# Matmuls on zeros at the head of an attention and MLP kernel: some bf16 ones exchanged for small float32 ones

## The chip, the cores and the metric

The kernel runs on one core of a Trainium2 chip. The metric is the device time of one execution in microseconds (us); the kernel before takes 675.98 us, the median of 3 runs (675.64 to 676.66). Profile times count from the first instruction of the profiled execution.

## The reference

Attention over 2 x 8 heads of 768 positions and 64 dimensions, in which a key counts for a query only if both fall in the same bucket (the signs of six projections), followed by two MLPs on the 1536 joined tokens:

```python
q_bits = (einsum('bhsd,dk->bhsk', q, proj) > 0); k_bits = (einsum('bhsd,dk->bhsk', k, proj) > 0)
mask = bucket(q_bits)[:, :, :, None] == bucket(k_bits)[:, :, None, :]
scores = where(mask, q @ k.T / sqrt(D), -1e9)
attn = exp(scores - max(scores)); attn = attn / (sum(attn) + 1e-9)
x = (attn @ v), heads joined to 512 columns
x = maximum(maximum(x @ w1, x @ w2), x @ w3) @ w_out
h = x @ w_in;  g = h where h >= 1, 0 where h <= -1, else (h + 1)**2 / 4
out = g @ w_out2
```

## The kernel before

Operands are split into a high and a low part, so that a float32 product becomes several products in TensorE's faster format. The attention comes first, in tiles of 128 queries by 768 keys, six to a head; then the MLPs, a long even stream of 128x512 matmuls (L867, L994).

A tile is computed by `t_qk` (L386 to L400): for each half of 384 keys a product of `qa` with `lo` (L395) and one of `qb` with `hi` (L398), into one half of a tile `s_ps`. VectorE takes the row maximum and copies (`t_max`, L402), ScalarE the exponential (`t_exp`, L416). In the odd heads and head 0 TensorE transposes the tile (`t_tr`, L425) into `t_ps` and multiplies it with V into `u_ps` (`g_pv`, L476). In the seven other heads, called turned, VectorE transposes 32x32 squares, and `block4` (L450) multiplies the whole head at once: 24 key blocks, each with four calls of 32 rows by 64 columns against 192 columns (L456, L457), which write to four places, one per group of 32 rows: `quarter(q)` is `u_ps`, the two halves of `t_ps`, and `pj_ps` (L447). `u_ps`, `pj_ps` and each half of `t_ps` are PSUM tiles of 128 x 512 float32.

The order of TensorE's work in the attention is written out by hand (L793 to L818); a planner places the other engines' work by costs and due times that it is given, and none of them comes from the matmuls on zeros. Each engine runs its own instructions in order.

The head of the kernel (L568 to L593) is apart from the planner. It issues the loads of head 0 and others on SyncE's queue, then 20 matmuls on zeros (`warm_up`, L285, a 128x256 bf16 tile `warm` by its first half), and prepares head 0: ScalarE makes `hi`, VectorE `lo`, TensorE multiplies with the projections (`bits_mm`, L368, rows 64 to 128 of `pj_ps` for the first half and of `u_ps` for the second), VectorE turns rows 64 to 108 of these into bits (`bits_rows`, L374), and VectorE and GpSimd move the parts to their rows (`prep_move`, L354). In the first tile `t_qk` puts 4 matmuls on zeros ahead of each L395 and 7 ahead of each L398 (L394, L397), written to the half of `t_ps` of the same number. Nothing reads what the matmuls on zeros write. All this is written under a manual schedule: the program keeps the written order on each engine, and waits are put in where one instruction touches what another has written or read.

At the end of the attention `g_fold_now` (L510) reads the two row halves of `u_ps` on two engines:

```python
nc.scalar.copy(out=pr["u"][DOWN, cs], in_=u_ps[UP, 0:HALF])            # L512
nc.vector.tensor_copy(out=pr["uc"][DOWN, cs], in_=u_ps[DOWN, 0:HALF])  # L513
```

Here `UP` is rows 0 to 64, `DOWN` rows 64 to 128, and `HALF` is 384.

Of the kernel before, what the change touches and what calls it, by code (L numbers as in the profile page):

```python
# [22 lines left out]
HALF = S // 2  # L23
# [90 lines left out]
def lsh_attention_moe_kernel(  # L114
# [14 lines left out]
    nc = tc.nc  # L129
# [20 lines left out]
    warm = const.tile([128, CH], BF16, name="warm")  # L150
# [5 lines left out]
    f32 = lambda ap: ap.bitcast(F32)  # L156
# [105 lines left out]
    def attention(mlp_steps):  # L262
        with ExitStack() as ax, ExitStack() as sx:
# [21 lines left out]
            def warm_up(count, i):  # L285
                for _ in range(count):
                    nc.tensor.matmul(out=t_ps[:, i, 0:CH], lhsT=warm[:, 0:128], rhs=warm, start=True, stop=True)


            def load_head(h, parts=1):  # L290
                r = raw_p.tile([128, S], F32, tag="r", name="r")
                for i in range(parts):
                    cs = slice(i * S // parts, (i + 1) * S // parts)
                    nc.sync.dma_start(out=r[:, cs], in_=kq[h, :, cs])
                    if parts > 1 and i == 0:
                        nc.sync.dma_start(out=pj_raw, in_=pj)
                head.setdefault(h, {})["r"] = r

            def load_v(h):
                vr = v_p.tile([128, NK, D], F32, tag="vr", name="vr", bufs=1)  # L300
                nc.sync.dma_start(out=vr, in_=v[h])
                head.setdefault(h, {})["vr"] = vr
# [45 lines left out]
            UP, DOWN = slice(0, 64), slice(64, 128)  # L348
# [37 lines left out]
            def t_qk(n, bank):  # L386
                h, t = divmod(n, NK)
                hd = head[h]
                qs = slice(t * 128, (t + 1) * 128)
                for half in range(2):  # L390
                    ks = slice(half * HALF, (half + 1) * HALF)
                    o = s_ps[bank.at][:, half, 0:HALF]
                    if n == 0:
                        warm_up(4, half)  # L394
                    nc.tensor.matmul(out=o, lhsT=hd["qa"][:, qs], rhs=hd["lo"][:, ks], start=True, stop=False)  # L395
                    if n == 0:
                        warm_up(7, half)  # L397
                    nc.tensor.matmul(  # L398
                        out=o, lhsT=hd["qb"][0:76, qs], rhs=hd["hi"][0:76, ks], start=False, stop=True
                    )  # L400
# [46 lines left out]
            def quarter(q):  # L447
                return (u_ps, t_ps[:, 0], t_ps[:, 1], pj_ps)[q]
# [118 lines left out]

            load_head(0, 2)  # L568
            nc.sync.dma_start(out=ident, in_=idn)
            warm_up(20, 0)  # L570
            load_v(0)
            load_head(1)
            banks0 = (pj_ps, u_ps)
# [97 lines left out]
            def tile_tasks(n):  # L671
# [4 lines left out]
                sp, pp = place("s", 1), place("p", 1 if turned else 2)  # L676
                takes = own(sums_p, "sums", h // 2, 1)
                qk = task("PE", 0.72, m, t_qk, n, sp, after=ready[h], takes=[sp], leaves=[h_place[h]])
                mx = task("DVE", 1.04, m, t_max, n, sp, after=[qk], takes=[pp], leaves=[sp])
                ex = task("ACT", 1.13, m, t_exp, n, after=[mx], takes=takes, lag=0.1)  # L680
# [342 lines left out]
    with tc.manual_schedule():  # L1023
        nc.scalar.dma_start(out=pc_sb, in_=pc)
        nc.vector.memset(half_sb, 0.5)
        nc.vector.memset(sc_sb[0:64], 1.0)
        nc.vector.memset(sc_sb[64:128], SCALE)
        mlp_steps = mlp()
        attention(mlp_steps)
        for _ in mlp_steps:  # L1030
            pass
# [42 lines left out]
```

## Time and profile before

| | |
|---|---|
| median of 3 runs | 675.98 us (675.64 to 676.66) |
| the profiled execution | 676.23 us, span 674.4 us from first to last instruction |
| TensorE | 662.3 us busy (98%), 4440 matmuls and as many weight loads |
| VectorE, ScalarE, GpSimd | 73%, 50%, 41% busy |
| attention, MLPs | to about 213 us, from there to the end |

In the timeline PE is TensorE's matmuls and PEld its weight loads; DVE is VectorE, ACT ScalarE, POOL GpSimd, SPq the issue of DMAs. A row gives start, duration and how many instructions were merged, then the engine, the line of the kernel and the tiles. The brackets give how long the engine stood idle before and what released it; "issue" means that it waited for nothing the profile shows. A matmul's duration goes on past the start of the next, as they are pipelined: the pace is read from the starts.

### The profile page before, as it was taken

The numbers are of one execution on the slowest core, as the hardware profiler recorded it, in microseconds if no ns is written. First come the engines' busy times: TensorE is split into PE (matmuls) and PEld (weight loads), VectorE is DVE, ScalarE is ACT, GpSimd is POOL, SyncE is SP. The second block draws the span as 40 slices with busy tenths as digits, with TensorE's granted clock in tenths as the row PEclk, the third lists the DMA queues.
The fourth block names the chain that finished last, engine by engine and source line by source line (L and its number), as shares of the span: only waits on it lengthen the run. The fifth ranks groups of instructions, "written<-read, shape, count | busy, mean of one in ns | idle before, by whom it ended". The sixth has DMA issues, their size and how long they took to land.

```text
span 674.4 us, 11567 instructions
## 1 busy us (share of the span) xinstructions
PE 662.3 (98%) x4440; PEld 530.3 (79%) x4440; DVE 492.3 (73%) x725; ACT 337.3 (50%) x625; POOL 273.4 (41%) x247
## 2 busy tenths in 40 slices
PE   8999999999999999999999999999999999999998
PEld 5667777677776888888888888888888888888886
DVE  6788889989962668777444366765888888888844
ACT  3686876887883233233222234765444444444430
POOL 4427448458322244354232123643444444444430
PEclk9999999999999999999999999999999999999999
DMA  4866777777431222221111121111222121111005
GB/s 126 218 163 159 200 190 208 206 193 180 108 118 49 94 94 94 95 88 52 52 56 33 63 94 62 63 63 33 66 76 73 67 64 63 63 63 62 33 0 188
DMA packets 27855, 66.99 MB, mean 99 GB/s; under 512 B 4164, under 2 KB 9124, under 8 KB 27800
## 3 DMA queue, kind: packets, MB, share of 16 engines
q1 hardware_dynamic: 27656, 66.25, 33.9%
q8 instruction: 35, 0.57, 0.3%
q14 instruction: 20, 0.16, 0.1%
q10 hardware_dynamic: 144, 0.00, 0.0%
HBM read 46.17 MB, written 3.19 MB: 73 GB/s over the span
## 4 chain that ended last, share of the span: by engine, by line
PE 94%; DVE 2%; DMA 2%; ACT 1%; issue 1%; SPq 0%; DVEq 0%; ACTq 0%
PE b L867 49%; PE b L994 19%; PE s_ps L395 5%; PE u_ps L480 5%; PE t_ps L428 5%; PE s_ps L398 4%; PE u_ps L456 3%; PE pj_ps L369 2%; PE t_ps L456 1%; DVE p L405 1%; DVE lo L329 1%; DMA r<-in_kq 1%; DMA rb<-d 0%; ACT pt L438 0%; PE pj_ps L456 0%
## 5 line engine op out<-in xcount | busy, mean ns | idle before, releaser
L867 PE MATMUL b<-x_hl,wx 128*128 128x512 f32 x684 | 159.6, 389 | 0.0
L867 PEld LDWEIGHTS b<-x_hl,wx 128*128 128x128 f32 x684 | 128.4, 188 | 26.7
L867 PE MATMUL b<-x_hl,w 128*128 128x512 f32 (+1 forms) x576 | 126.8, 376 | 0.0
L867 PEld LDWEIGHTS b<-x_hl,w 128*128 128x128 f32 x576 | 103.1, 188 | 20.7 <-issue 0.6
L894 POOL TENSOR_TENSOR g<-r,g 128x512 fp32r<-128x512 f32 x48 | 62.5, 1304 | 121.4 <-ACT g L893 121.4
L405 DVE TENSOR_SCALAR_CACHE_REDUCE p<-s_ps 128x768 f32<-128x768 f32 x96 | 89.6, 950 | 11.8 <-PE s_ps L398 9.4
L420 ACT ACTIVATE p<-p,nm 128x768 f32<-128x768 f32 x96 | 89.7, 935 | 12.3 <-DVE p L405 11.6
L205 DVE SCALAR_TENSOR_TENSOR wg<-wg,wr 128x512 f32<-128x512 f32 (+1 forms) x58 | 67.3, 1160 | 36.6 <-ACT wg L203 35.8
L395 PE MATMUL s_ps<-lo,q 128*128 128x384 f32 x192 | 72.0, 375 | 2.8 <-DVE p L405 2.7
L232 POOL TENSOR_TENSOR wx<-wg,wx 128x512 fp32r<-128x512 f32 (+1 forms) x32 | 45.6, 1425 | 65.4 <-ACT wx L226 48.5
L994 PE MATMUL b<-wx,g 128*128 128x512 f32 x288 | 72.1, 389 | 0.0
L994 PE MATMUL b<-w,g 128*128 128x512 f32 (+1 forms) x294 | 71.3, 385 | 0.0
L398 PE MATMUL s_ps<-hi,q 76*128 76x384 f32 x192 | 65.4, 341 | 0.5 <-DVE hi L360 0.3
L226 ACT CAST wx<-wg 128x512 fp32r<-128x512 f32 (+1 forms) x32 | 19.4, 605 | 92.7 <-DVE wg L218 88.6
L974 DVE SCALAR_TENSOR_TENSOR r<-r,b 128x512 f32<-128x512 f32 x48 | 33.0, 688 | 44.4 <-ACT r L973 44.4
L994 PEld LDWEIGHTS b<-w,g 128*128 128x128 f32 x294 | 54.5, 188 | 11.1
L994 PEld LDWEIGHTS b<-wx,g 128*128 128x128 f32 x288 | 54.0, 188 | 11.2
L1001 DVE TENSOR_TENSOR acc<-b,acc 128x512 f32<-128x512 f32 (+1 forms) x85 | 56.3, 675 | 7.7 <-PE b L994 7.6
L232 POOL TENSOR_TENSOR w<-wg,w 128x512 fp32r<-128x512 f32 (+1 forms) x26 | 36.0, 1384 | 58.3 <-ACT w L226 48.1
L210 DVE TENSOR_SCALAR wg<-wg 128x512 int32<-128x512 int32 (+1 forms) x58 | 54.3, 936 | 2.7
L972 ACT ACTIVATE r<-b,half_sb 128x512 f32<-128x512 f32 x48 | 33.0, 687 | 41.2 <-PE b L867 41.2
L226 ACT CAST w<-wg 128x512 fp32r<-128x512 f32 (+1 forms) x26 | 15.8, 609 | 74.2 <-DVE wg L218 74.2
(84 smaller groups left out, 1064.5 us busy)
## 6 DMA issues: line engine op xcount, KB each, us to landing
wr<-in_w SPq DMA_DIRECT2D x48, 512.0 KB
r<-in_kq SPq DMA_DIRECT2D x15, 384.0 KB
q<-hi SPq DMA_DIRECT2D x15, 384.0 KB
v<-in_v SPq DMA_DIRECT2D x21, 256.0 KB
rb<-d SPq DMA_DIRECT2D x16, 192.0 KB
wr<-in_w SPq DMA_DIRECT2D x8, 384.0 KB
q<-lo SPq DMA_DIRECT2D x15, 192.0 KB
lo<-hi SPq DMA_DIRECT2D x15, 192.0 KB
```

Source lines behind the costliest of these rows:

```text
L205: nc.vector.scalar_tensor_tensor(out=f32(g), in0=f32(g), scalar=TINY_SQ, in1=f32(high), op0=ALU.is_ge, op1=ALU.mult)
L210: nc.vector.tensor_scalar(out=g2, in0=g, scalar1=3, scalar2=0x3FFFFFF8, op0=ALU.logical_shift_left, op1=ALU.bitwise_and)
L226: nc.scalar.copy(out=w[:, 0, 0:cols], in_=f32(g2))
L232: nc.gpsimd.tensor_tensor(out=w[:, 1, 0:cols], in0=f32(g2), in1=f32(w[:, 0, 0:cols]), op=ALU.subtract)
L395: nc.tensor.matmul(out=o, lhsT=hd["qa"][:, qs], rhs=hd["lo"][:, ks], start=True, stop=False)
L398: nc.tensor.matmul(out=o, lhsT=hd["qb"][0:76, qs], rhs=hd["hi"][0:76, ks], start=False, stop=True)
L405: nc.vector.tensor_scalar(out=p.rearrange("p (a k) -> p a k", a=2), in0=s_ps[bank.at][:, :, 0:HALF], scalar1=MASKED, scalar2=MASKED, op0=A ...
L420: nc.scalar.activation(out=p, in_=p, func=ACTF.Exp, scale=-1.0, bias=tl[n]["nm"], accum_out=sums_of(h // 2)[:, c:c + 1],)
L867: nc.tensor.matmul(out=outp, lhsT=w_[a], rhs=x_[b_], start=(i == 0 and jj == 0), stop=(i == n - 1 and jj == 2),)
L894: nc.gpsimd.tensor_tensor(out=dst[:, 1, cs], in0=src, in1=f32(dst[:, 0, cs]), op=ALU.subtract)
L994: nc.tensor.matmul(out=pb[:, cs], lhsT=gs[f][:, a, tsl], rhs=wt[:, b_, cs], start=(n == 0), stop=(n == len(terms) - 1),)
L1001: nc.vector.tensor_tensor(out=acc[:, t, cs], in0=pb[:, cs], in1=acc[:, t, cs], op=ALU.add)
```

## The change

The 20 matmuls on zeros of the opening become 10, followed by 14 rounds of small float32 ones. In the first tile 4 rounds stand in place of each 4, and 5 rounds in place of each 7. A round is four calls, one per group of 32 rows, each with 64 columns against 64 columns of the zero tile read as float32. They write rows 0 to 64, columns 448 to 512, of `u_ps`, of the halves of `t_ps`, and of `pj_ps`. There are 446 more TensorE instructions ahead of the first turned block. Nothing else changes.

```diff
+            def warm_small(rounds):
+                zeros = f32(warm)
+                for _ in range(rounds):
+                    for q in range(4):
+                        rows = slice(32 * q, 32 * q + 32)
+                        nc.tensor.matmul(
+                            out=quarter(q)[UP, HALF + 64:512], lhsT=zeros[rows, 0:64], rhs=zeros[rows, 64:128],
+                            start=True, stop=True,
+                        )
...
                     if n == 0:
-                        warm_up(4, half)
+                        warm_small(4)
                     nc.tensor.matmul(out=o, lhsT=hd["qa"][:, qs], rhs=hd["lo"][:, ks], start=True, stop=False)
                     if n == 0:
-                        warm_up(7, half)
+                        warm_small(5)
...
             nc.sync.dma_start(out=ident, in_=idn)
-            warm_up(20, 0)
+            warm_up(10, 0)
+            warm_small(14)
             load_v(0)
```

## Rows read from the trace of the kernel before

**Rows 1.** The page, the chain that ended last: share of the span by engine.

```profile
PE 94%; DVE 2%; DMA 2%; ACT 1%; issue 1%; SPq 0%; DVEq 0%; ACTq 0%
```

**Rows 2.** The chain in order of time, head: start us, us, what.

```profile
9.22 0.41 PE s_ps L398
...
11.26 0.74 DVE p L405
```

**Rows 3.** The timeline of the head: start us, us, engine, line, what.

```profile
1.06 4.45 PE L287 MATMUL t_ps<-warm 128*128 128x256 bf16 x20 [1.06 <-DVE warm L151]
...
5.43 1.34 PE L369 MATMUL pj_ps<-r,pj_sc 128*64 128x384 f32 x2
...
6.61 0.81 PE L369 MATMUL u_ps<-r,pj_sc 128*64 128x384 f32 x2
...
7.35 0.61 PE L287 MATMUL t_ps<-warm 128*128 128x256 bf16 x4
...
7.93 0.69 DVE L376 TENSOR_SCALAR q<-pj_ps,pc_sb 44x384 fp32r<-44x384 f32 x1
...
9.50 0.69 DVE L376 TENSOR_SCALAR q<-u_ps,pc_sb 44x384 fp32r<-44x384 f32 x1
...
10.80 0.42 PE L398 MATMUL s_ps<-hi,q 76*128 76x384 f32 x1
...
16.80 0.45 PE L395 MATMUL s_ps<-lo,q 128*128 128x384 f32 x1 [1.78 <-DVE p L405]
```

**Rows 4.** The timeline of TensorE's matmuls around the second turned block.

```profile
85.17 0.33 PE L398 MATMUL s_ps<-hi,q 76*128 76x384 f32 x1
85.43 0.37 PE L456 MATMUL u_ps<-dt,v 32*64 32x192 f32 x1
...
89.27 0.32 PE L456 MATMUL pj_ps<-dt,v 32*64 32x192 f32 x1
89.52 0.44 PE L395 MATMUL s_ps<-lo,q 128*128 128x384 f32 x1
```

**Rows 5.** Windows from the start: length, busy us (count) of PE, PEld, DVE, ACT, POOL; clock, DMA.

```profile
0.00:61.20 61.20, 56.27 (x331) 38.79 (x331) 48.54 (x92) 40.15 (x79) 25.27 (x35) 1.00 0.65 170
0.00:64.06 64.06, 59.13 (x470) 41.61 (x471) 51.20 (x98) 42.52 (x84) 28.05 (x38) 1.00 0.64 165
...
0.00:85.42 85.42, 80.18 (x640) 56.84 (x640) 68.55 (x128) 58.36 (x115) 39.49 (x51) 1.00 0.67 173
0.00:109.80 109.80, 104.18 (x955) 74.64 (x955) 89.38 (x165) 77.13 (x152) 53.65 (x67) 1.00 0.70 182
0.00:134.02 134.02, 128.03 (x1258) 92.64 (x1258) 111.47 (x204) 95.65 (x189) 69.13 (x83) 1.00 0.71 184
0.00:157.66 157.66, 151.67 (x1567) 110.41 (x1567) 132.32 (x242) 114.75 (x226) 84.67 (x99) 1.00 0.72 187
0.00:182.10 182.10, 175.56 (x1876) 128.45 (x1876) 154.65 (x280) 133.26 (x263) 96.11 (x112) 1.00 0.70 181
0.00:205.57 205.57, 197.49 (x2179) 145.23 (x2179) 170.67 (x311) 151.91 (x301) 105.39 (x122) 1.00 0.65 170
```

**Rows 6.** The chain in order of time, after the first turned block.

```profile
66.20 0.37 PE s_ps L395
...
67.11 0.66 PE t_ps L428 x6
```

**Rows 7.** The timeline of TensorE's weight loads inside the first turned block.

```profile
64.69 0.13 PEld L456 LDWEIGHTS t_ps<-dt,v 32*64 32x64 f32 x1 [0.66 <-issue]
```

**Rows 8.** The page's DMA queues: the instruction queue, packets, MB, share of 16 engines.

```profile
q8 instruction: 35, 0.57, 0.3%
```

**Rows 9.** The instructions of L287: duration ns min/median/max, first and last start.

```profile
L287 PE MATMUL t_ps<-warm x42: 272/283/417, 1.1 to 10.8; 128*128 128x256 bf16 x42
```

**Rows 10.** The timeline at the end of the attention, the two reads of `u_ps`.

```profile
214.26 0.47 ACT L512 COPY u<-u_ps 64x384 f32<-64x384 f32 x1 [2.28 <-DMA uc<-u]
...
214.82 0.56 DVE L513 COPY uc<-u_ps 64x384 f32<-64x384 f32 x1 [10.41 <-ACT u L512]
```

## The prediction

> **What bounds the kernel now.** I read the page's chain first: 94% of it is TensorE [rows 1], so time that TensorE loses in the attention stage tends to stay lost. The change touches only the first twelve microseconds and the position of everything later in TensorE's instruction stream, so I read those two places.
>
> In the head the chain runs through VectorE and ends in TensorE [rows 2]: the second product of the first tile's first half starts at 9.22, more matmuls on zeros and products follow, and the first row maximum on VectorE starts at 11.26. The timeline [rows 3] gives the rest. VectorE reads the bits out of `pj_ps` (from 7.93) and out of `u_ps` (9.50 to 10.19); the last product of the first tile starts at 10.80. Today's matmuls on zeros write only `t_ps`, which nobody has read by then, so they wait for nobody.
>
> For the stream: the blocks of L456 (turned heads) are the only stretch with hundreds of short instructions. A block is 192 loads and 192 matmuls. The second runs from 85.43 to the next product at 89.52, 4.09 us [rows 4]. The first begins at 61.20, after 331 matmuls and 331 loads [rows 5], and the next product starts at 66.20 [rows 6], 5.0 us; in it the weight loads wait 0.66 us for nothing but issue, until 64.69 [rows 7]. Queue 8 carries instructions: 35 packets, 0.57 MB, so 16 KB each [rows 8], for 8,880 loads and matmuls, one per 253.7. I read the gap as a late packet.
>
> **Part 1, the opening.** Ten of the twenty matmuls go: (4.45 - 0.42) / 19 = 0.212 us each [rows 3, 9], 2.1 us. In come 14 rounds of 4 float32 calls. One float32 call is two matmuls (the one bit call on `u_ps` shows x2 [rows 3]), so 112 load-matmul pairs. No row shows a pair this small. Lower bound: a block's pace, (89.27 - 85.43) / 191 = 20.1 ns for 192 columns [rows 4], of which 64 columns are a third, 6.7 ns. Upper bound: that pace unscaled, 20 ns. The nearest row where the load is as long as the matmul: six 128-column transposes in 0.66 us [rows 6], 0.11 each; half of it for 64 columns and a quarter for four row groups side by side is some 13.5 ns, which I take. In the opening TensorE is at its lower level: 0.212 us a matmul there, (0.61 - 0.28) / 3 = 0.11 at 7.35 [rows 3, 9], so 1.2 against 2.4 GHz. There the pair is 27 ns and 112 are 3.0 us. The bit products then start 0.9 us later. I count nothing for it: their results lie ready at some 6.8 and 7.4, and are read at 7.93 and 9.50. Were a pair 40 ns there, the first read would slip by some 1.2 us.
>
> **Part 2, a new wait.** The rounds inside the first tile write four places, among them `u_ps` and `pj_ps`, rows 0 to 64, columns 448 to 512. VectorE's reads of the bits use rows 64 to 108 of the same two tiles and stand earlier in the program. Does a write wait for a read of other rows of its tile? The end of the attention answers: ScalarE reads rows 0 to 64 of `u_ps` at 214.26 for 0.47 us, and VectorE reads rows 64 to 128 only at 214.82, after 10.41 us idle put down to ScalarE [rows 10]. Even two reads of different rows stand in line there. So the first small matmul of the tile (it goes to `u_ps`) waits for the read that ends at 10.19 and starts at about 10.3, and TensorE, in order, holds all four products of tile 0 behind it. Behind those wait VectorE's first row maximum, the first exponential, and what follows on them.
>
> The stated count fits: 128 calls x 2 x 2 = 512 instructions in, 32 x 2 = 64 out, makes 448; 446 leaves two fewer, as when waits of the products on VectorE become needless.
>
> Its price: four bursts now run after 10.3, where only the last product had to. Their spans are 2 x (31 + 39) x 13.5 ns = 1.9 us. Entering a burst costs 0.26 us (85.17 to 85.43), leaving it 0.25 (89.27 to 89.52) [rows 4]; 3 entries and 4 exits are 1.78. The last product starts at 10.3 + 3.7 = 14.0 instead of 10.80: **+3.2 us**. With 6.7 and 20 ns it would be 10.3 + 0.94 + 1.78 and 10.3 + 2.8 + 1.78, so the bounds are +2.2 and +4.1. The first maximum, the link by which the chain leaves the head [rows 2], hangs on that product, so I pass it on in full. No DMA is added or moved.
>
> **Part 3, the stream moves.** The gap at 64.69 comes after 470 matmuls and 471 loads, 941 in all; the seven blocks begin after 662, 1280, 1910, 2516, 3134, 3752 and 4358 [rows 5]. Packet edges lie 253.7 apart, counted from the gap. So an edge falls 25, 168, 46, 201, 90, 233 and 135 into the blocks. Where it falls before some 130, the next edge is still inside the 384 of the block, with no slow work to cover its packet: blocks 1, 3 and 5 should stop, 2, 4, 6 and 7 not. The two blocks read above agree, 5.0 and 4.09 us, so a stop costs 0.9. With 446 more ahead the edges lie 446 - 512 = -66 from where they were, that is 66 later in each block: 91, 234, 112, 13, 156, 45, 201. Now blocks 1, 3, 4 and 6 stop, four for three: **+0.9 us**. If the edge at 13 falls ahead of its block, or only a part of a stop is passed on, it is less. Bounds: -0.9 and +1.8, a stop fewer or two more.
>
> The Trainium skill ("Runtime: NRT & Kernel Launch", Instruction fetch mechanics) says that blocks of 256 instructions are fetched ahead and that the crossing is mostly hidden. The packet size agrees with the trace; the gap of 0.66 us inside a dense block does not. By the page the sum would lose this part and give 679.2.
>
> The sum: the profiled execution took 676.23 us, a span of 674.4 and 1.8 around it, 0.25 above the median of 675.98. 676.23 + 3.2 + 0.9 = 680.3; at the level of the median, **680.1 us**.
>
> **Rivals.**
> (a) No wait: accesses to different rows of a tile don't stand in line. For it: the row at 214.82 is one case, with two readers and no writer. Against: that row. Then the second product stays at 9.22, the next starts at 9.22 + 0.26 + 31 x 13.5 ns + 0.25 = 10.15, and the last at 10.15 + 0.26 + 39 x 13.5 ns + 0.25 = 11.19, 0.39 after 10.80; at 6.7 ns it would be 10.70, no loss. With part 3: 675.98 + 0.4 + 0.9 = 677.3, and 676.3 where no stop is added: not measurably slower. It decides if the first small matmul of the tile starts well before 10.2. 17%. The Trainium skill ("PSUM — Partial Sum Buffer", PSUM bank collisions raise a hardware error) holds that accesses exclude each other only in one bank and one 32-row quadrant, which would allow this rival; no row here shows it.
> (b) The wait, and the clock falls in it. TensorE would stand idle from some 8.3 to 10.3. Before 16.80 it idled 1.78 us, and the product after it took 0.45 us, no doubling [rows 3]; a longer pause is not shown. At 1.2 GHz bursts and products double: +1.9 + 0.5, so 682.5. 13%.
> (c) Faster: no wait, and packets come sooner, so that no block stops: 675.98 - 3 x 0.9 = 673.3. Against: every packet would have to come some 0.66 us sooner. 4%.
> The forecast has 66%: the wait, at full clock.
>
> **Range and chances.** A measurement of this kernel can tell 0.2%, 1.35 us: faster is below 674.6, slower above 677.3. The forecast and (b) are slower, 79%, and 3% of (a), where the stop counts in full; the other 14% of (a) are the same; (c) is faster. The forecast's own bounds are 675.98 + 2.2 - 0.9 = 677.3 and 675.98 + 4.1 + 1.8 = 681.9. Up to (b) and down to most of (a) makes 676.7 to 682.6.
>
> **What would show it.** Right: the first small matmul inside tile 0 starts at 10.3, released by VectorE's read of `u_ps`; the first row maximum at about 14.5 instead of 11.26; blocks 1, 3, 4 and 6 last about 5.0 us, the others 4.1. Part 1 is wrong if the 56 calls of the opening take far from 3.0 us or VectorE waits for the bit products. Part 2 is wrong if small matmuls of the tile run from 8 on, and its passing on if the delay at 60 us is not that at 14. Part 3 is wrong if other blocks stop.

## The result, and the profile after

The changed kernel takes **680.93 us** (median of 8 runs, 677.67 to 682.85) beside 676.17 us of the kernel before (8 runs, 675.27 to 678.87): 4.76 us or 0.7% slower, ratio 1.0068 with a 95% interval of 1.0051 to 1.0085. The profiled execution took 680.27 us with a span of 678.5, against 676.23 and 674.4: +4.1 in the span. Its mean granted TensorE clock is 0.992, where the one before had 1.000. Of the eight executions seven lie between 0.989 and 0.992 (680.17 us and more); the eighth has 1.000, and that is the one of 677.67 us. One execution of the experiments below, of the kernel without the wait, took 1110.74 us at a mean granted clock of 0.557 and is left out of that kernel's median.

First the page of the kernel after: queue 8 (packets, MB, share), and the chain that ended last, by engine and then by line.

```profile
q8 instruction: 36, 0.59, 0.4%
...
PE 96%; DVE 2%; ACT 1%; issue 1%; DMA 0%; DVEq 0%; ACTq 0%
PE b L878 48%; PE b L1005 19%; PE s_ps L405 6%; PE t_ps L438 5%; PE u_ps L490 5%; PE s_ps L408 5%; PE u_ps L466 3%; PE pj_ps L379 2%; PE t_ps L466 1%; PE u_ps L294 1%; ACT pt L448 0%; DVE p L415 0%; PE pj_ps L466 0%; DMA r<-in_kq 0%; DVE q L386 0%
```

The chain [rows 1] has gained two links: L294, the small matmuls themselves, with 1% of the span, and the bit reads of L386. There is one instruction packet more than before [rows 8]. Next the head: the timeline of TensorE's matmuls.

```profile
3.46 0.31 PE L294 MATMUL u_ps<-warm 32*64 32x64 f32 x1
...
3.89 0.31 PE L294 MATMUL u_ps<-warm 32*64 32x64 f32 x1
...
4.16 0.22 PE L294 MATMUL u_ps<-warm 32*64 32x64 f32 x1
...
5.26 0.22 PE L294 MATMUL u_ps<-warm 32*64 32x64 f32 x1
...
5.42 0.86 PE L379 MATMUL pj_ps<-r,pj_sc 128*64 128x384 f32 x2
6.12 0.81 PE L379 MATMUL u_ps<-r,pj_sc 128*64 128x384 f32 x2
10.15 0.27 PE L294 MATMUL u_ps<-warm 32*64 32x64 f32 x1 [3.22 <-DVE q L386]
...
10.77 0.59 PE L405 MATMUL s_ps<-lo,q 128*128 128x384 f32 x1
...
12.56 0.69 PE L408 MATMUL s_ps<-hi,q 76*128 76x384 f32 x1
...
16.14 0.69 PE L408 MATMUL s_ps<-hi,q 76*128 76x384 f32 x1
```

Three things are to be seen. The bit products start at 5.42, where they did before (5.43) [rows 3]. Then TensorE stands still for 3.22 us, until VectorE has read `u_ps`; the predicted wait. And the last of the first tile's four products (the third is at 14.24) starts at 16.14 and not at 14.0 as predicted, 5.3 us after its old place. The same stretch on VectorE, where the row maxima (L415) are what the chain goes through:

```profile
9.41 0.69 DVE L386 TENSOR_SCALAR q<-u_ps,pc_sb 44x384 fp32r<-44x384 f32 x1
...
16.86 0.96 DVE L415 TENSOR_SCALAR_CACHE_REDUCE p<-s_ps 128x768 f32<-128x768 f32 x1 [5.71 <-PE s_ps L408]
...
19.14 1.15 DVE L339 SCALAR_TENSOR_TENSOR lo<-r,sc_sb,hi 128x384 fp32r<-128x384 f32 x2
21.20 0.96 DVE L415 TENSOR_SCALAR_CACHE_REDUCE p<-s_ps 128x768 f32<-128x768 f32 x1 [0.91 <-PE s_ps L408]
```

Why the tile took so long stands in the windows (window, then busy us and count of PE, PEld, DVE, ACT, POOL, then the granted clock, the DMA share and GB/s):

```profile
8.00:10.00 2.00, 0.00 (x0) 0.00 (x0) 1.85 (x4) 0.26 (x1) 0.70 (x2) 1.00 0.76 229
10.00:12.00 2.00, 1.85 (x60) 1.46 (x63) 1.05 (x2) 0.00 (x0) 1.74 (x3) 0.73 0.90 195
12.00:14.00 2.00, 2.00 (x56) 1.55 (x52) 0.00 (x0) 0.00 (x0) 1.87 (x2) 0.50 0.23 88
...
18.00:20.00 2.00, 2.00 (x6) 0.79 (x6) 1.83 (x4) 1.75 (x4) 0.00 (x0) 0.50 0.00 0
20.00:22.00 2.00, 2.00 (x12) 1.91 (x12) 1.09 (x2) 0.26 (x3) 0.00 (x0) 0.71 0.31 65
```

From 8 to 10 TensorE does nothing. Soon after it starts again, at 10.9, its granted clock falls to 0.50, which is 1.2 of 2.4 GHz, and it is back only at some 21.1 (a mean of 0.71 in the window from 20 leaves 1.16 us of it at half; 10.9 comes from the 0.73 in the same way). The last small matmul starts at 15.89, so for some 5 us more the clock is low with the ordinary products alone. The profile of the kernel before shows 1.00 throughout. The last view is block 1's entry and the stops inside blocks, in the timeline of the weight loads:

```profile
66.69 0.13 PEld L466 LDWEIGHTS u_ps<-dt,v 32*64 32x64 f32 x1 [0.25 <-issue]
...
71.38 0.13 PEld L466 LDWEIGHTS t_ps<-dt,v 32*64 32x64 f32 x1 [1.22 <-issue]
...
119.70 0.13 PEld L466 LDWEIGHTS t_ps<-dt,v 32*64 32x64 f32 x2 [0.35 <-issue]
```

Block 1 starts at 66.69, and blocks 1 and 3 are the only ones with a stop inside. In the kernel before, beside the 0.66 in block 1 [rows 7], blocks 3 and 5 had these, in the same view:

```profile
113.62 0.13 PEld L456 LDWEIGHTS t_ps<-dt,v 32*64 32x64 f32 x2 [0.72 <-issue]
...
162.03 0.13 PEld L456 LDWEIGHTS t_ps<-dt,v 32*64 32x64 f32 x2 [0.90 <-issue]
```

An account of the two profiled executions, at points that both have:

| point | before | after | later by |
|---|---|---|---|
| first row maximum | 11.26 | 16.86 | 5.6 |
| third row maximum | 15.79 | 21.20 | 5.4 |
| block 1 | 61.21 | 66.69 | 5.5 |
| block 7 | 205.58 | 209.81 | 4.2 |
| span | 674.4 | 678.5 | 4.1 |

Block 7 is counted from its third matmul: in both executions its first two start 0.96 us ahead, and the others wait for a copy by ScalarE. So the head loses 5.5 us, and between blocks 1 and 7 1.3 us come back. I call a block's excess what it takes from its first to its last matmul beyond the 3.83 us of an undisturbed one: before, blocks 1, 3 and 5 had 0.83 + 0.90 + 1.08 = 2.8; after, blocks 1 and 3 have 1.39 + 0.53 = 1.9. That is 0.9 of the 1.3.

### The profile page after: what moved, and what is told of

Its sections match the earlier page's. It is cut to its first block, busy times and chain, and to the rows that moved or that the text cites. A ratio compares the mean times of both kernels' runs of the same rounds, so it can differ in the third digit from the quotient of the medians.

```text
span 678.5 us, 12013 instructions
## 1 busy us (share of the span) xinstructions
PE 665.8 (98%) x4664; PEld 534.2 (79%) x4664; DVE 490.6 (72%) x725; ACT 337.3 (50%) x625; POOL 272.8 (40%) x247
## 4 chain that ended last, share of the span: by engine, by line
PE 96%; DVE 2%; ACT 1%; issue 1%; DMA 0%; DVEq 0%; ACTq 0%
PE b L878 48%; PE b L1005 19%; PE s_ps L405 6%; PE t_ps L438 5%; PE u_ps L490 5%; PE s_ps L408 5%; PE u_ps L466 3%; PE pj_ps L379 2%; PE t_ps L466 1%; PE u_ps L294 1%; ACT pt L448 0%; DVE p L415 0%; PE pj_ps L466 0%; DMA r<-in_kq 0%; DVE q L386 0%
## 5 line engine op out<-in xcount | busy, mean ns | idle before, releaser
L415 DVE TENSOR_SCALAR_CACHE_REDUCE p<-s_ps 128x768 f32<-128x768 f32 x96 | 89.8, 951 | 17.9 <-PE s_ps L408 14.5
```

The lines of the kernel that those rows point to most:

```text
L415: nc.vector.tensor_scalar(out=p.rearrange("p (a k) -> p a k", a=2), in0=s_ps[bank.at][:, :, 0:HALF], scalar1=MASKED, scalar2=MASKED, op0=A ...
```

## The experiments

The theory after the result: the wait on the read of `u_ps` puts TensorE to rest, the rest costs it the clock, and the small matmuls behind it keep the clock low. The rivals: the small matmuls cost this much by themselves wherever they write; the wait alone, at full clock, does it; the moved stream does it. Ratios are to the kernel before on the same chip, whose medians in the three groups of runs were 675.49, 675.82 and 675.64 us.

**No wait, the same small matmuls.** In the first tile the rounds write places that VectorE has not read.

```diff
+            def unread(q):
+                return (s_ps[1][:, 0], t_ps[:, 0], t_ps[:, 1], s_ps[1][:, 1])[q]
...
-                        warm_small(4)
+                        warm_small(4, unread)
...
-                        warm_small(5)
+                        warm_small(5, unread)
```

> The changed kernel, but inside tile 0 the small matmuls write to s_ps of the second tile in place of u_ps and pj_ps, which nobody has read by then: same number, size and place in the order, no wait. Theory A (the wait on VectorE's read of u_ps, and the clock that falls in the pause): first small matmul of the tile well before 10, last product of tile 0 at 11.0 to 11.4, granted clock 1.00 from then on, time 675 to 676.5 us. Theory B (the small matmuls cost by themselves, in bursts and in going in and out of them): 679 to 681 us, last product past 13. Theory C (the moved instruction stream costs it): 680 to 681 us, with the head as fast as before.

Measured: 674.82 us (median of nine executions), ratio 0.9997 (0.9978 to 1.0015). The timelines of this kernel's matmuls and of VectorE:

```profile
6.50 0.86 PE L382 MATMUL pj_ps<-r,pj_sc 128*64 128x384 f32 x2
...
7.93 0.27 PE L294 MATMUL s_ps<-warm 32*64 32x64 f32 x1
...
12.25 0.96 DVE L418 TENSOR_SCALAR_CACHE_REDUCE p<-s_ps 128x768 f32<-128x768 f32 x1 [1.56 <-PE s_ps L411]
```

The first small matmul follows the bit products at once, at 7.93, and the first maximum comes at 12.25 instead of 16.86. The places decide: by themselves the small matmuls cost the first maximum 1.0 us and the end nothing that the interval can tell. I had expected the clock to stay at 1.00, but in this profiled execution it fell at 20.1, after pauses that have nothing to do with the change's wait: 1.39 us ahead of 17.37, and 0.95 us ahead of 19.96. Timeline and window:

```profile
19.96 1.45 PE L441 MATMUL t_ps<-ident,p 128*128 128x128 f32 x6 [0.95 <-ACT pt L451]
```

```profile
20.00:22.00 2.00, 2.00 (x9) 2.00 (x10) 1.10 (x2) 0.83 (x2) 1.20 (x2) 0.52 0.65 182
```

It was low for 3.4 us. Executions of this kernel at a mean clock of 1.000 took 673.7 to 676.0 us, those at 0.995 to 0.997 took 676.3 to 678.4.

**The wait alone.** The kernel before, with the first of the first tile's matmuls on zeros written to `u_ps`.

```diff
+                    if n == 0 and half == 0:
+                        nc.tensor.matmul(out=u_ps[UP, HALF + 64:512], lhsT=warm[:, 0:64], rhs=warm[:, 0:64], start=True, stop=True)
                     if n == 0:
-                        warm_up(4, half)
+                        warm_up(4 - (half == 0), half)
```

> The kernel before, with one of its bf16 matmuls on zeros (the first of tile 0) written to rows 0 to 64, columns 448 to 512 of u_ps: the wait alone, no small matmuls, no moved stream. Theory A: it starts at about 10.2; last product of tile 0 at 13.3 if the clock stays (678.5 us) and at 16.2 if it falls (681.4 us). Theory B and theory C: 676.2 us, as before.

Measured: 678.98 us, ratio 1.0046 (1.0029 to 1.0062). Timeline of its matmuls, then its windows:

```profile
10.40 0.21 PE L394 MATMUL u_ps<-warm 128*64 128x64 bf16 x1 [2.90 <-DVE q L376]
...
14.71 0.42 PE L400 MATMUL s_ps<-hi,q 76*128 76x384 f32 x1
```

```profile
10.00:12.00 2.00, 1.60 (x8) 1.01 (x8) 0.70 (x2) 0.00 (x0) 1.12 (x2) 0.51 0.87 227
12.00:14.00 2.00, 2.00 (x12) 1.43 (x10) 0.00 (x0) 0.00 (x0) 1.92 (x3) 0.64 0.32 105
```

One write to rows that VectorE's read leaves out makes TensorE wait 2.90 us. Here too the clock falls, in the pause itself, but for 3.4 us (10.0 to 13.4), not 10.2; large matmuls stand behind it. All four executions have a mean clock of 0.997. The last product, 14.71, lies between the two starts that I had expected, 13.3 at full clock and 16.2 at half.

**The pause filled.** The kernel after, with 32 bf16 matmuls on zeros into `t_ps` where TensorE would wait, and four rounds fewer in the opening, so that the instruction count stays.

```diff
+                    if n == 0 and half == 0:
+                        warm_up(32, 0)
...
-            warm_small(14)
+            warm_small(10)
```

> The changed kernel with 32 bf16 matmuls on zeros into t_ps ahead of the first small one of tile 0, so that TensorE does not pause between the bit products and 10.1, and 10 rounds for 14 in the opening, so that the stream moves by the same 446. Theory A: the small ones still start at about 10.2, granted clock 1.00 throughout, last product at 13.6 to 14.2, time 677.0 to 678.3 us. If the fall of the clock is beside the point: 680.5 to 681 us.

Measured: 676.87 us, 0.1 below what I had expected, ratio 1.002 (1.0007 to 1.0033), and a clock of 0.999 or 1.000 in all ten executions. Timelines of TensorE's matmuls and weight loads, VectorE and GpSimd, then a window:

```profile
6.61 3.67 PE L287 MATMUL t_ps<-warm 128*128 128x256 bf16 x32
...
14.14 0.44 PE L410 MATMUL s_ps<-hi,q 76*128 76x384 f32 x1
...
62.94 0.13 PEld L468 LDWEIGHTS u_ps<-dt,v 32*64 32x64 f32 x1 [0.24 <-issue]
...
14.62 0.96 DVE L417 TENSOR_SCALAR_CACHE_REDUCE p<-s_ps 128x768 f32<-128x768 f32 x1 [3.68 <-PE s_ps L410]
...
16.50 1.15 DVE L339 SCALAR_TENSOR_TENSOR lo<-r,sc_sb,hi 128x384 fp32r<-128x384 f32 x2
17.56 0.95 DVE L417 TENSOR_SCALAR_CACHE_REDUCE p<-s_ps 128x768 f32<-128x768 f32 x1
...
11.71 1.95 POOL L356 TENSOR_TENSOR lo<-r,hi 128x384 fp32r<-128x384 f32 x2
```

```profile
10.00:12.00 2.00, 1.97 (x76) 1.42 (x73) 0.84 (x2) 0.00 (x0) 1.85 (x3) 1.00 0.95 203
```

This is the forecast's case, the wait at full clock: the products start at 10.93, 12.04, 13.03 and 14.14, the first maximum at 14.62. Against the kernel before of its own runs it loses 1.4 us (676.87 - 675.49), the kernel after 4.76: the fall of the clock costs some 3.4 us. The executions of the kernel after say 3.3 (680.93 - 677.67). It also shows how little of the wait is left at the end: the first maximum is 3.4 us late, the third (17.56 for 15.79) 1.8, block 1 (62.94 for 61.21) 1.7. What came back between the first and the third is VectorE's low part. In the kernel before it ran beside GpSimd's, in the timelines of these two engines:

```profile
13.14 2.73 DVE L329 SCALAR_TENSOR_TENSOR lo<-r,sc_sb,hi 128x384 fp32r<-128x384 f32 x2
15.79 0.94 DVE L405 TENSOR_SCALAR_CACHE_REDUCE p<-s_ps 128x768 f32<-128x768 f32 x1
...
13.17 2.28 POOL L346 TENSOR_TENSOR lo<-r,hi 128x384 fp32r<-128x384 f32 x2
```

Both start at 13.1 and VectorE's pair takes 2.73 us. With the pause filled GpSimd, which also started 1.5 us sooner, is done at 13.7, and with the maxima late VectorE's pair starts only at 16.50 and takes 1.15: 1.6 us less, which is 3.4 - 1.8. The Trainium skill ("SBUF — State Buffer", SBUF: two separate sides) says that a VectorE operation with two inputs from SBUF and a GpSimd operation that reads SBUF exclude each other for a whole instruction; the two durations agree.

**The opening alone.** The kernel after, with the first tile as before (`warm_up(4, half)`, `warm_up(7, half)`); 204 instructions ahead instead of 446.

```diff
-                        warm_small(4)
+                        warm_up(4, half)
...
-                        warm_small(5)
+                        warm_up(7, half)
```

> The changed opening (10 bf16, 14 rounds of small ones), but tile 0 with the bf16 matmuls of before: stream moved by some 204. Theory A: row maximum of tile 0 at about 11.3 as before, clock 1.00, and what is left is the stream: 675 to 676.5 us. Theory B: between 676 and 678 us, according to the number of small ones left (56 calls of 128). Theory C: 679 to 681 us.

Measured: 674.90 us, 0.1 below what I had expected, ratio 0.9987 (0.9978 to 0.9996). VectorE's timeline:

```profile
11.30 0.96 DVE L415 TENSOR_SCALAR_CACHE_REDUCE p<-s_ps 128x768 f32<-128x768 f32 x1 [0.62 <-PE s_ps L408]
```

First maximum at 11.30, third at 15.77, as before: the opening costs the first tiles nothing (block 1 starts at 61.72, 0.5 us later). The slowdown is all in the first tile. The small gain fits the stream's: stops of 0.30, 0.57 and 0.68 in blocks 1, 3 and 6, where the kernel before has 2.8 us of them. Four of the ten executions stand at a clock of 0.997 although no wait was added.

**The stream's phase.** As the last, with other counts in the opening: 12 bf16 matmuls and 9 rounds put 128 instructions more ahead of block 1, 12 and 17 put 256, 6 and 15 put 212.

```diff
-            warm_up(10, 0)
-            warm_small(14)
+            warm_up(12, 0)
+            warm_small(9)
```

> The kernel before with an opening of 12 bf16 matmuls and 9 small rounds: TensorE's stream moved by 128 instructions, half a packet, and nothing else. Theory of the packets (a block stops where an edge falls some 15 to 125 instructions into it): the stops leave blocks 1, 3 and 5 and come up in blocks 2, 4 and 6 (edges at about 35, 65 and 95), so these are 4.3 us and longer from first to last matmul start and 1, 3 and 5 are 3.84. Rival (a block is slow by its own place or by the DMAs beside it): 1, 3 and 5 stay the slow ones. Time 674.5 to 676.5 us by either.

> The same with 12 bf16 matmuls and 17 rounds: 256 instructions more, one whole packet. Theory of the packets: the edges lie in the blocks where they lay before, so blocks 1, 3 and 5 stop as before, and the time is that of before, 675 to 676.2 us. Rival (the number of instructions, not the phase): a pattern of its own.

> The same with 6 bf16 matmuls and 15 rounds: 212 more, the phase with the fewest edges in the first part of a block (about 62, 91, 122 and 9 in blocks 1, 3, 5 and 6). Theory of the packets: two stops, in 1 and 3, and at most a short one in 5; 674.2 to 675.2 us, 0.3 to 1.2 below before.

The timeline of weight loads with 128 more, first row block 1's entry, and then with 256 more:

```profile
60.56 0.13 PEld L466 LDWEIGHTS u_ps<-dt,v 32*64 32x64 f32 x1 [0.25 <-issue]
...
88.39 0.13 PEld L466 LDWEIGHTS t_ps<-dt,v 32*64 32x64 f32 x2 [1.28 <-issue]
...
136.59 0.14 PEld L466 LDWEIGHTS t_ps<-dt,v 32*64 32x64 f32 x2 [0.29 <-issue]
...
184.54 0.13 PEld L466 LDWEIGHTS u_ps<-dt,v 32*64 32x64 f32 x1 [0.73 <-issue]
```

```profile
113.36 0.13 PEld L466 LDWEIGHTS t_ps<-dt,v 32*64 32x64 f32 x2 [0.86 <-issue]
...
162.63 0.13 PEld L466 LDWEIGHTS t_ps<-dt,v 32*64 32x64 f32 x2 [1.09 <-issue]
```

Half a packet on, the stops move from blocks 1, 3 and 5 to 2, 4 and 6; a whole packet on, they are in 1, 3 and 5 again. The mechanism of packet edges holds. The times: 674.28 us (0.9989, 0.997 to 1.0009) with 128, 676.90 (1.0013, 0.9996 to 1.003) with 256, whose first maximum was also 0.6 late, and 674.08 (0.9981, 0.9967 to 0.9995) with 212, where three short stops cost 1.2 us in all. All three lie outside the times that I had expected, the second above, the others below. The last is the lowest of the counts tried, but not told apart from that with 128.

The stops alone do not explain these times. With 128 more they add up to 2.7 us, nearly what the kernel before has, yet its median is 1.5 us below. In its profile and in that with 212 more the third maximum comes early, at 15.15 and 15.32 for 15.79: GpSimd's low part started 0.7 and 0.5 us sooner than in the kernel before, and VectorE's pair beside it took 1.91 and 2.14 us, not 2.73. How much of either gain is the stream's stays open.

Edges counted from these runs (with TensorE's other instructions counted too; good to some 2) and excess of each block, edge first. The edge is the first that falls into the block; a stop comes at the next, some 256 instructions on.

| kernel | block 1 | 2 | 3 | 4 | 5 | 6 | 7 |
|---|---|---|---|---|---|---|---|
| before | 20: 0.83 | 163: 0 | 49: 0.90 | 193: 0 | 80: 1.08 | 223: 0 | 131: 0 |
| after | 86: 1.39 | 229: 0 | 115: 0.53 | 3: 0 | 146: 0 | 33: 0 | 197: 0 |
| pause filled | 86: 0.63 | 229: 0 | 115: 0.82 | 3: 0 | 146: 0 | 33: 0.60 | 197: 0 |
| 128 more | 148: 0 | 35: 1.47 | 177: 0 | 65: 0.48 | 208: 0 | 95: 0.75 | 3: 0 |
| 212 more | 64: 0.38 | 207: 0 | 93: 0.34 | 237: 0 | 126: 0.47 | 11: 0 | 175: 0 |

Edges from 19 (block 6 of the opening alone) to 126 can stop a block, edges at 3 and 11 or from 131 on did not. How long a stop is, the edge does not say: 86 cost 1.39 and 0.63, and 33 cost 0 and 0.60.

**The wait, with large matmuls behind the new opening.** The opening alone, and the first tile as in the wait alone.

```diff
+                    if n == 0 and half == 0:
+                        nc.tensor.matmul(out=u_ps[UP, HALF + 64:512], lhsT=warm[:, 0:64], rhs=warm[:, 0:64], start=True, stop=True)
...
-                        warm_small(4)
+                        warm_up(4 - (half == 0), half)
```

> The changed opening, and in tile 0 the bf16 matmuls of before with the first of them written to u_ps: the wait and the pause of the changed kernel, but large matmuls behind the pause in place of the small ones; stream moved by some 204. If the small matmuls behind the pause keep the granted clock at its lower level for long (10.2 us in the changed kernel): it is low for about 3.4 us here, as with the wait alone, the first row maximum starts at about 15.2 and not 16.9, and the time is 677.5 to 678.8 us. If the opening with small matmuls is the cause: low for about 10 us, 679.5 to 681 us.

Measured: 676.08 us, ratio 1.001 (0.9997 to 1.0023); I had expected too much. A window, and the waiting matmul in the timeline:

```profile
10.00:12.00 2.00, 1.79 (x15) 1.38 (x15) 0.51 (x2) 0.00 (x0) 0.20 (x1) 1.00 1.03 281
```

```profile
10.21 0.19 PE L404 MATMUL u_ps<-warm 128*64 128x64 bf16 x1 [2.21 <-DVE q L386]
```

In this execution the bits were done at 8.0, the pause was 2.21 us, and the clock did not fall; block 1 started at 62.13, 0.9 us later than in the kernel before. Six of ten executions stand at 1.000 (675.5 to 676.1 us), four at 0.997 (676.6 to 677.8), none near 0.99. But four of ten stood at 0.997 in the opening alone too, so this run does not show that the wait makes the clock fall. Among the profiles the long stretch at 0.50 was seen only with small matmuls behind the wait. The mean clocks show that a fall can come without it: 6 of the 79 executions of the kernel before in these three groups lie at 0.949 to 0.997, and one of the kernel with 128 more at 0.992 (680.06 us). In the kernel after it is seven of eight.

**Low parts apart.** Since the two low parts disturb each other, I let VectorE make its own earlier, by the planner's due time, on top of the opening alone; then together with the phase of 212.

```diff
-            SHIFT = {..., prep_lo_scaled: -3.0, ...}
+            SHIFT = {..., prep_lo_scaled: -8.0, ...}
```

> The opening of the run before (10 bf16, 14 rounds, bf16 in tile 0), and the planner's due time of VectorE's low part of head 1 moved ahead, so that VectorE makes it before the first two row maxima and not beside GpSimd's low part of head 2. If the 1.6 us that VectorE's work lost or won there is a slowdown from working beside GpSimd: the two low parts take about 1.2 us and not 2.7, the third row maximum starts at 13.7 to 14.5 and not at 15.8, and the time is 673 to 674.3 us. If their length has another cause: 2.7 us wherever they stand, and 674.5 to 676 us.

> The stream moved by 212 (6 bf16 matmuls and 15 rounds in the opening, bf16 in tile 0) together with VectorE's low part of head 1 ahead of the first two row maxima. If the two gains add: 673.0 to 674.0 us, a ratio to before of 0.996 to 0.998. If they only replace each other: as either alone, 674.1 to 674.6 us.

Measured: 674.36 us (0.997, 0.995 to 0.9989) alone, 675.41 (0.9993, 0.9978 to 1.0009) together. VectorE's timeline of the first, then of the second:

```profile
10.82 1.72 DVE L339 SCALAR_TENSOR_TENSOR lo<-r,sc_sb,hi 128x384 fp32r<-128x384 f32 x2
...
15.15 0.96 DVE L415 TENSOR_SCALAR_CACHE_REDUCE p<-s_ps 128x768 f32<-128x768 f32 x1
```

```profile
11.32 2.34 DVE L339 SCALAR_TENSOR_TENSOR lo<-r,sc_sb,hi 128x384 fp32r<-128x384 f32 x2
```

The pair took 1.72 us in the first, as GpSimd's scaling ran beside it, so the third maximum came at 15.15, 0.6 early and not the 1.3 or more I had hoped for. In the second GpSimd's low part had also moved earlier (12.06, for 2.46 us), the pair took 2.34, and the third maximum came at 16.27; block 3 stopped for 1.10 where the same edge had cost 0.34. The gains do not add; the two together lie above either expectation. The kernels with the phase of 212 and with the low part earlier each beat the kernel before, by 0.2% and 0.3%, and so the kernel after. The second contains the new opening, which alone gave 0.1%, and the two intervals overlap: what the earlier low part adds is not shown apart.

## Why the prediction was right and wrong

The sign held, and the time lay in the range. That the sum came within 1 us is luck: its likeliest case, the wait at full clock, is not what seven of eight executions did, and two errors of some 2 us, a head too cheap and a stream too dear, nearly cancel.

**Part 1, the opening: no cost, right; its length missed.** 3.0 us were predicted for its 56 calls and 2.0 measured. The price of a pair was right: 0.43 us for 16 pairs from 3.46 to 3.89 is 27 ns (27 predicted), 1.10 us for 76 pairs from 4.16 to 5.26 is 14.5 ns (13.5 predicted). What failed was taking the lower level for the whole opening: the pace changes at some 4.1. The view's 1.00 ahead of that is no measurement: the trace's records of the granted clock begin only at 4.08, and in the profiles with the pause filled and with the opening alone they begin, and the pace changes, at 4.56 and 6.06. In the kernel without the wait they begin at 6.44, the opening ran at the lower level to its end, and the bits start at 6.50, as the 3.0 us would have it. So when the bits start varies by 1.1 us, and with it the pause behind them.

**Part 2, the new wait: right; its price wrong twice.** The first small matmul started at 10.15 (10.3 predicted), released by the read of `u_ps`, and the kernel with other places shows that it hangs on the place. The failing step is the one that made the forecast's clock: "Before 16.80 it idled 1.78 us, and the product after it took 0.45 us, no doubling", with the pause put at 2.0 us and a fall of the clock at 13%. The pause was 3.22, since the bits were done at 6.93 and not 8.3, and the clock fell in seven executions of eight. Rival (b) was the usual case, and its price of +2.4 us was too low as well. It doubled only the bursts and products of the first tile; the clock stayed low until 21.1, through the second tile and the third, for which VectorE waits until 21.20. Measured, the fall costs some 3.4 us. The pause is not all that decides: 2.21 us in the last run with a wait went without a fall, and the clock of the kernel without the wait fell after 0.95. The Trainium skill ("TensorE: Matmul & The Clock Gate", HAM oscillation — how this bites in real kernels) says that a long enough wait for data costs TensorE its full clock, and that the work behind it starts cold; the windows from 8 to 22 agree but for the first 0.75 us of that work, which ran before the fall, and the rule should have weighed more than one row with a shorter pause.

The other failing step is "I pass it on in full". With the pause filled, the last product came at 14.14 (14.0 predicted) and the first maximum at 14.62 (14.5), but 1.7 us were left at block 1, as VectorE's low part no longer met GpSimd's. The whole kernel then lost 1.4 us. The one execution after the change at a clock of 1.000, at +1.5, fits. So the likeliest case, had it come alone, would have given some 677.4 us (675.98 + 1.4), not 680.1.

**Part 3, the stream: mechanism right, count wrong.** "Now blocks 1, 3, 4 and 6 stop": blocks 1 and 3 did. The edge at 13 was at 3, and an edge that early did not stop a block in any run; the prediction named that doubt. The one at 45 was at 33, which sometimes stops and sometimes not. "A stop costs 0.9" was the other error: stops run from 0.3 to 1.5. So the term is -0.9 where +0.9 was forecast, the lower end of its bounds. Two slips in the working change no block that it names: the count ahead of block 3 is 1898 and not 1910, as the window ends just behind the block's start, and the shift of 66 goes by packets of 256 where the edges go by 253.7.

The sum by what was measured, in the profiled executions: +5.5 at block 1, -0.9 of stops, and some -0.5 that I could not place: +4.1. Forecast were +3.2 and +0.9. Rival (a), no wait, fell with the first row of the wait; rival (c) fell in its no-wait part, though the stream did gain.

Still open: why the clock of the opening rises at 4.1 in one execution and after 6 in another; why it stays low for 10.2 us behind the small matmuls, the last 5 of them with ordinary products, where with large ones it was back in 3.4; why it falls after one pause and not after another; and what sets the length of a stop at a given edge. That the one execution at a clock of 1.000 was one with a slow opening, and so a shorter pause, would fit, but no profile of it was taken.

## What to carry to other kernels

Work on zeros that is to keep TensorE busy must write places that nobody has read shortly before: the wait it inherits can rest TensorE long enough to cost more in clock than in waiting. Price a new wait by following it to the next point where two engines meet, as a delay can pull apart work that was in each other's way and give half of itself back. Where instruction packets are late, changing the count of instructions ahead of a dense block moves the stops, but their length scatters by about 1 us.

## What the runs showed of the hardware

- A wait between a read of rows 64 to 108 and a write of rows 0 to 64 of one PSUM tile: TensorE stood 2.2 to 3.2 us here, in the kernel after and in both with a single large write. The program puts such waits in; no run shows whether the hardware needs this one.
- The clock after a pause: with a pause of 3.22 us the granted clock fell to 0.50 at 10.9, 0.75 us after work resumed, and with one of 2.90 at 10.0, 0.4 us before. With pauses of 2.21 and 1.78 it stayed at 1.00 in the profiled executions, and after one of 0.95, with one of 1.39 shortly before, it fell. It stayed at 0.50 for 10.2 us where small float32 matmuls, each on 32 rows, and then ordinary products stood behind the pause, for 3.4 with large bf16 ones, though TensorE was busy for 2.00 of 2.00 us in windows of both.
- VectorE's pair of low parts: 1.15 us alone, 1.72 beside GpSimd's scaling, 1.90 to 2.73 where it met GpSimd's low part.
